# Which engine evicts the outputs: ScalarE in fixed stretches of the loop, VectorE elsewhere, and a branch hint on one more engine

## The chip, the core and the metric

The kernel runs on one core of a Trainium2 chip. Its engines are TensorE (PE; its weight loads are listed as PEld), VectorE (DVE), ScalarE (ACT), GpSimd (POOL) and SyncE (SP, which here issues nearly all transfers). The metric is the device time of one execution in microseconds. Three runs of the kernel before took 461.12, 462.41 and 466.04 us; their median is 462.41 us.

## The reference

Four batches of 12480 tokens with 128 features attend twice over 32 inducing points, and the result goes through a two-layer network with a squared ReLU. Cut to what is computed:

```python
def mab(q, kv):
    s = (q @ kv.transpose(0, 2, 1)) / sqrt(128)
    a = exp(s - s.max(-1, keepdims=True))
    a /= a.sum(-1, keepdims=True) + 1e-09
    return a @ kv
h = mab(I, x)                 # I: 32 inducing points, the same for all batches
y = mab(x, h)                 # so each row of y is a mixture of the 32 rows of h[b]
out = maximum(y @ w_in, 0) ** 2 @ w_out      # w_in 128x2048, w_out 2048x128
```

## The kernel before, in words

Since a row of y is a mixture of 32 rows, the kernel does not carry 2048 hidden columns per token. For each batch it turns the weights into a small quadratic form in the 32 attention weights: `prepare` (19 steps) computes `hw` (L466), the products `G` (L518), the sums `wq` on TensorE (L527), which `evac` writes to the batch's weights `w16` (L175 on ScalarE or L179 on VectorE), the linear part `lin` and `bias` (L591). These weights are "a batch's weights" below.

Four pieces of work run beside each other, batch by batch:

- `first(b)`: the first attention. Scores go to `sT` with their maximum (L298), the maxima are folded (`m` L305, a transposition `mt` on TensorE L307, `gm` L309, `gm` copied L311, a broadcast by TensorE `mb` L314, `nb` L316), `exp` on ScalarE (L323), a transposition `en` (L333), and `hacc` on TensorE (L345), which reads x once more from DRAM through five `xnb` buffers. `hq` (L351, L353) sums, and `hT` is done.
- `prepare(b)`, as above, needs `hT`.
- `second(b, G)`, seven groups per batch: scores, softmax on VectorE, GpSimd (L387, L394) and ScalarE (L388), then the 16-bit copy `a16` (L404 on ScalarE or L406 on VectorE) and its remainder (L407, VectorE), stored to DRAM.
- `squares(b, G)`: reads those back as `dT`, and adds squares `zz` (`sq` L442, `z` L448 on VectorE, L452 on GpSimd, stored into `dT` by L454).

The main loop goes over 104 chunks, 26 per batch, each of 480 columns. A chunk has four TensorE products into two double banks, `up` (L638, `hp`), two squarings on ScalarE of 128x960, `lift` (L647, `g`), and in the next round `down`: four products with `w16` and one with `lin` into one bank (`po`, L653 and L654, two buffers), the eviction of the bank with scale and bias to `o` (three buffers), and the store of `o` (L660). The eviction is L657 on ScalarE or L659 on VectorE. `g` has three buffers, so lifts can be at most three chunks ahead of `down`.

Which engine evicts is set by `to_act`: two running sums, `held["act"]` and `held["dve"]`, collect estimated nanoseconds of the work that was given to each engine, and a piece goes to ScalarE when its sum stays lower. The same test decides `a16` and the `w16` evictions. With it, ScalarE evicts 44 chunks and VectorE 60:

```
batch 0  chunks 0-25 ScalarE
batch 1  0-2 ScalarE, 3-7 VectorE, 8-19 ScalarE, 20-25 VectorE
batch 2  0-7 VectorE, 8-9 ScalarE, 10-14 VectorE, 15 ScalarE, 16-25 VectorE
batch 3  0-25 VectorE
```

The order of the background work is a plan: every step of the four pieces has a due time in chunks (`head` is the due time at which `prepare(b)` begins: -3.5, 13.9, 35 and 61), and `background` issues what is due after each lift. A scheduler (`schedule_with_timeline_sim`) then orders the instructions of each engine by its own estimate of durations. The engines run their lists in order.

At the end a flag is loaded on every engine (L933) and a branch (L934) skips a long other way of computing, "whole".

## Time and profile before

| what | value |
|---|---|
| runs, us | 461.12, 462.41, 466.04 |
| the profiled execution's own time | 464.73 us |
| its span, first to last instruction | 463.0 us |
| mean granted TensorE clock | 0.934 |
| VectorE busy | 325.7 us |
| ScalarE busy | 282.0 us |
| one output eviction, ScalarE / VectorE | 762 ns / 763 ns |
| the 60 evictions on VectorE | 45.4 us |
| the 44 evictions on ScalarE | 33.0 us |
| one lift of 128x960 | 974 ns |

The table's rows are totals over the span, and the limits differ along it. The text therefore reads stretches: for each batch the time from `hw` to the last `w16` (the "weights stage"), the stretch in which `first` streams x, and the last stretch, in which only chunks are left. In a chain of waits, "issue" is time in which nothing was waited for that the profile shows.

### The profile page before, as it was taken

Reading aid. Unit: us, or ns where it says so; the run is one execution under the profiler, and the core shown is the slowest. Engines: PE = TensorE matmul, PEld = TensorE weight load, DVE = VectorE, ACT = ScalarE, POOL = GpSimd, SP = SyncE. Lnnn points to the kernel's source line nnn. Section 1 sums busy time; section 2 is a strip of 40 time slices with the busy share of each in tenths; the row PEclk is TensorE's granted clock in tenths of the full one; section 3 lists DMA queues with packets and bytes.
Section 4 is the critical chain, followed back from the end, with each engine's and each line's share of the span. In section 5 each row is a group of like instructions: output and inputs, shape, how many; then the busy total and the mean of one; then the engine's idle time right before and its main releaser. Section 6 shows DMA issues by size and latency. Waiting matters only on the chain.

```text
span 463.0 us, 8566 instructions
## 1 busy us (share of the span) xinstructions
PE 366.8 (79%) x2979; PEld 163.2 (35%) x2979; DVE 325.7 (70%) x902; ACT 282.0 (61%) x397; POOL 85.9 (19%) x93
## 2 busy tenths in 40 slices
PE   0644744899979889878789888988879898788994
PEld 0003413543335333333244234433433344343441
DVE  8969378685643199497561899689626999996442
ACT  1004123479994497437567798566666878067993
POOL 1000011141210030232200132144100423340000
PEclk9999975699979799799599999999999999999998
DMA  7999980377759983667889958644794354337432
GB/s 296 421 248 392 372 295 24 97 240 249 207 173 337 335 277 101 197 188 187 266 276 293 344 195 244 195 138 145 240 290 154 102 167 165 101 128 231 151 136 105
DMA packets 64771, 100.71 MB, mean 218 GB/s; under 512 B 22992, under 2 KB 53968, under 8 KB 64720
## 3 DMA queue, kind: packets, MB, share of 16 engines
q1 hardware_dynamic: 64720, 100.09, 66.3%
q8 instruction: 25, 0.41, 0.4%
q14 instruction: 26, 0.21, 0.1%
HBM read 64.91 MB, written 31.95 MB: 209 GB/s over the span
## 4 chain that ended last, share of the span: by engine, by line
PE 30%; DVE 28%; DMA 26%; ACT 6%; issue 5%; SPq 2%; POOL 1%; ACTq 0%; DVEq 0%; POOLq 0%
DMA xnb<-xn_dram 8%; PE hp L638 8%; PE po L653 7%; ACT g L647 5%; DMA outT_dram<-o 5%; PE s L264 4%; PE hacc L345 4%; DMA xp_False<-xT_dram 4%; DMA dT<-zz 3%; DVE o L659 3%; DVE G L518 3%; DVE a L407 2%; PE wq L527 2%; DMA wo<-w_out_dram 2%; DMA dT<-ad 2%
## 5 line engine op out<-in xcount | busy, mean ns | idle before, releaser
L647 ACT ACTIVATE g<-hp 128x960 f16<-128x960 f32 x208 | 194.4, 974 | 60.7 <-PE hp L638 48.2
L638 PE MATMUL hp<-dT,pairs 96*128 96x480 f16 x416 | 121.4, 381 | 7.3 <-ACT g L647 4.9
L653 PE MATMUL po<-g,w 128*128 128x480 f16 x416 | 115.8, 377 | 7.6 <-ACT o L657 3.4
L387 POOL TENSOR_TENSOR e<-e,mx 128x480 f32<-128x480 f32 (+1 forms) x28 | 28.0, 999 | 232.2 <-DVE mx L383 76.3
L659 DVE TENSOR_SCALAR o<-po,osc,bias 128x480 f32<-128x480 f32 x60 | 45.4, 763 | 30.5 <-PE po L654 17.8
L653 PEld LDWEIGHTS <-w 128*128 128x128 f16 x416 | 40.6, 100 | 60.7 <-issue 19.3
L638 PEld LDWEIGHTS <-pairs 96*128 96x128 f16 x416 | 35.8, 101 | 66.6 <-issue 42.1
L345 PE MATMUL hacc<-xnb,en 128*32 128x128 f32 x784 | 38.3, 324 | 16.8 <-DMA xnb<-xn_dram 8.7
L264 PE MATMUL s<-xp_False,indT_sb 128*32 128x480 f32 (+1 forms) x224 | 32.9, 665 | 22.4 <-DMA xp_False<-xT_dram 12.1
L654 PE MATMUL po<-dT,lin 128*128 128x480 f16 x104 | 39.1, 379 | 7.7 <-DMA dT<-zz 7.5
L452 POOL TENSOR_TENSOR zz<-z 128x480 f16<-128x480 f32 (+1 forms) x28 | 30.2, 1078 | 66.3 <-DVE z L448 39.8
L323 ACT ACTIVATE sT<-sT,nb 128x480 f32<-128x480 f32 (+1 forms) x28 | 18.2, 658 | 33.5 <-DVE nb L316 33.5
L394 POOL TENSOR_TENSOR e<-e,z 128x480 f32<-128x480 f32 (+1 forms) x28 | 27.0, 967 | 56.1 <-DVE z L393 36.9
L345 PEld LDWEIGHTS hacc<-xnb,en 128*32 128x32 f32 x784 | 24.4, 126 | 33.6 <-DMA xnb<-xn_dram 9.7
L657 ACT ACTIVATE o<-po,bias,osc 128x480 f32<-128x480 f32 x44 | 33.0, 762 | 5.2 <-DMA outT_dram<-o 4.4
L353 DVE TENSOR_TENSOR hq<-hacc,hq 128x128 f32<-128x128 f32 x24 | 7.0, 291 | 37.6 <-PE hacc L345 37.6
L264 PE MATMUL s<-xp_False,hT 128*32 128x480 f32 (+1 forms) x224 | 27.7, 563 | 4.3 <-DVE k L195 1.4
L448 DVE TENSOR_SCALAR z<-sq,off,cut 128x480 f32<-128x480 f32 (+1 forms) x28 | 21.5, 767 | 9.3 <-PE sq L442 9.3
L518 DVE TENSOR_TENSOR G<-hwp,hw 128x512 f16<-128x512 f16 x64 | 24.9, 455 | 4.1 <-PE wq L527 4.1
L388 ACT ACTIVATE e<-e 128x480 f32<-128x480 f32 (+1 forms) x28 | 16.2, 578 | 17.0 <-POOL e L387 17.0
L404 ACT ACTIVATE a<-a,lessen 128x480 f16<-128x480 f32 (+1 forms) x20 | 13.6, 681 | 16.5 <-DVE a L397 16.3
L298 DVE TENSOR_SCALAR_CACHE_REDUCE sT<-s 128x480 f32<-128x480 f32 (+1 forms) x28 | 17.0, 608 | 9.1 <-PE s L264 9.1
(190 smaller groups left out, 419.2 us busy)
## 6 DMA issues: line engine op xcount, KB each, us to landing
outT_dram<-o SPq DMA_DIRECT2D x104, 240.0 KB, 2.8
xp_False<-xT_dram SPq DMA_DIRECT2D x24, 960.0 KB, 6.8
xnb<-xn_dram SPq DMA_DIRECT2D x28, 448.0 KB, 5.2
xnb<-xn_dram SPq DMA_DIRECT2D x24, 512.0 KB, 5.9
dT<-ad SPq DMA_DIRECT2D x72, 120.0 KB, 2.6
ad<-a SPq DMA_DIRECT2D x24, 240.0 KB, 2.5
dT<-zz SPq DMA_DIRECT2D x104, 30.0 KB, 2.3
wi<-w_in_dram SPq DMA_DIRECT2D x4, 512.0 KB, 5.6
```

What stands on the lines that cost most here:

```text
L264: nc.tensor.matmul(ps[32 * q:32 * q + 32, 0:w], lhsT, xp[:, w * q:w * q + w], start=True, stop=True,)
L345: st.last = nc.tensor.matmul(hacc[32 * q:32 * q + 32, 0:P], en[:, t], xg[:, t % 8], start=t < 4, stop=t + 4 >= nb32,)
L387: nc.gpsimd.tensor_tensor(e[:, 0:t], e[:, 0:t], mx[:, 0:t].unsqueeze(2).broadcast_to([P, t, MI]), op=ALU.subtract)
L394: nc.gpsimd.tensor_tensor(e[:, 0:t], e[:, 0:t], z[:, 0:t].unsqueeze(2).broadcast_to([P, t, MI]), op=ALU.mult)
L452: nc.gpsimd.tensor_tensor(g[rows], zv[rows], zv[rows], op=ALU.mult)
L518: tt(g[:, :, MI * j:MI * j + n], hwp[:, :, 0:n], hw16f[:, :, s0:s0 + n], op=ALU.mult)
L638: nc.tensor.matmul(hp[:, i, 0:CH].rearrange("p (q t) -> p q t", q=4), pairs[0:96, (2 * j + i) * P:(2 * j + i + 1) * P], self.dT[0:96], sta ...
L647: nc.scalar.activation(self.g[:, 2 * j:2 * j + 2], self.hp.pop(j)[:, 0:2, 0:CH], AF.Square)
L653: nc.tensor.matmul(po[:, 0:CH], st.w16[:, i], self.g[:, i], start=i == 0, stop=False)
L654: done = [nc.tensor.matmul(po[:, 0:CH].rearrange("p (q t) -> p q t", q=4), st.lin, self.dT, start=False, stop=True)]
L657: nc.scalar.activation(o, po[:, 0:CH], AF.Identity, bias=st.bias, scale=st.osc)
L659: done.append(nc.vector.tensor_scalar(o, po[:, 0:CH], st.osc, st.bias, op0=ALU.mult, op1=ALU.add))
```

## The change

`down` no longer asks `to_act`, it is told. A chunk is "heavy" if its number lies in one of the stretches of 18 chunks that begin at a batch's `head`, that is in -3.5 to 14.5, 13.9 to 31.9, 35 to 53 or 61 to 79; heavy chunks are evicted by ScalarE, all others by VectorE, and the very last by ScalarE. The evictions no longer enter the two sums, so the test for `a16` and `w16` comes out differently too: of the 28 `a16` copies 26 instead of 20 are on ScalarE, and all 16 `w16` evictions instead of 13. The list of instructions that get the branch hint now begins with the lift, so ScalarE gets one as well.

```diff
+HEAVY = 18
...
-            nc.scalar.activation(self.g[:, 2 * j:2 * j + 2], self.hp.pop(j)[:, 0:2, 0:CH], AF.Square)
+            return nc.scalar.activation(self.g[:, 2 * j:2 * j + 2], self.hp.pop(j)[:, 0:2, 0:CH], AF.Square)
...
-        def down(self):
+        def down(self, act):
...
-            if to_act(220 + 0.833 * CH, 110 + 1.042 * CH):
-                nc.scalar.activation(o, po[:, 0:CH], AF.Identity, bias=st.bias, scale=st.osc)
+            if act:
+                done.append(nc.scalar.activation(o, po[:, 0:CH], AF.Identity, bias=st.bias, scale=st.osc))
...
-    plan = []
+    plan, busy = [], []
+
+    def heavy(n):
+        return any(a <= n < z for a, z in busy)
...
+        busy.append((head, head + HEAVY))
...
-            chunk.lift(j)
+            done = [chunk.lift(j)]
...
-                done = chunks[n - 1].down()
+                done += chunks[n - 1].down(heavy(n - 1))
...
-    chunks[-1].down()
+    chunks[-1].down(True)
```

The engines' evictions after the change:

```
batch 0  chunks 0-25 ScalarE
batch 1  0-5 ScalarE, 6-8 VectorE, 9-25 ScalarE
batch 2  0 ScalarE, 1-8 VectorE, 9-25 ScalarE
batch 3  0 ScalarE, 1-24 VectorE, 25 ScalarE
```

ScalarE has 69 of them and VectorE 35. Up to chunk 2 of batch 1 nothing moves on any engine. Three places where the lists differ follow.

On VectorE, in batch 1 where `first` of batch 2 folds its maxima (`o_3` and `o_4` are the outputs of chunks 3 and 4, `gm` the folded maxima, `mx`, `z` and `e` belong to the last groups of `second`). Before:

```order
L391 TENSOR_REDUCE z_1_5_2243<-e_1_5_2202 128x15
L659 TENSOR_SCALAR o_3_2517<-po_3_2511,osc_157,bias_158 128x480
L381 STREAM_TRANSPOSE e_1_6_2285<-s_1_6_2279 128x256
L309 TENSOR_REDUCE gm_2293<-mt_2291 1x32
L392 TENSOR_SCALAR z_1_5_2243<-z_1_5_2243 128x15
L383 TENSOR_REDUCE mx_1_6_2287<-e_1_6_2285 128x8
L311 COPY gm_2_2295<-gm_2293 1x128
L393 RECIPROCAL z_1_5_2243<-z_1_5_2243 128x15
L659 TENSOR_SCALAR o_4_2567<-po_4_2561,osc_157,bias_158 128x480
L448 TENSOR_SCALAR z_2_2407<-sq_2_2402,off_153,cut 128x480
L316 TENSOR_SCALAR nb<-mb_2301 128x1
```

and after:

```order
L392 TENSOR_REDUCE z_1_5_2243<-e_1_5_2202 128x15
L382 STREAM_TRANSPOSE e_1_6_2285<-s_1_6_2279 128x256
L310 TENSOR_REDUCE gm_2293<-mt_2291 1x32
L393 TENSOR_SCALAR z_1_5_2243<-z_1_5_2243 128x15
L384 TENSOR_REDUCE mx_1_6_2287<-e_1_6_2285 128x8
L312 COPY gm_2_2295<-gm_2293 1x128
L394 RECIPROCAL z_1_5_2243<-z_1_5_2243 128x15
L449 TENSOR_SCALAR z_2_2407<-sq_2_2402,off_153,cut 128x480
L317 TENSOR_SCALAR nb<-mb_2301 128x1
```

The two evictions ahead of and behind `gm` are gone from this list. On TensorE, `mb` also moves: it stood behind the products `hp_6_0` and the first two of `po_5`, and now stands ahead of them.

On ScalarE at the same place, up to the exponentials `sT` of `first` of batch 2. Before:

```order
L647 ACTIVATE g_4_2506<-hp_4_1_2483 128x960
L657 ACTIVATE o_2_2456<-po_2_2450,bias_158,osc_157 128x480
L647 ACTIVATE g_5_2556<-hp_5_0_2508 128x960
L647 ACTIVATE g_5_2556<-hp_5_1_2540 128x960
L647 ACTIVATE g_6_2583<-hp_6_0_2558 128x960
L388 ACTIVATE e_1_6_2285<-e_1_6_2285 128x256
L647 ACTIVATE g_6_2583<-hp_6_1_2580 128x960
L323 ACTIVATE sT_1809,zs_2321<-sT_1809,nb 128x480 x6
```

and after:

```order
L648 ACTIVATE g_4_2506<-hp_4_1_2483 128x960
L658 ACTIVATE o_2_2456<-po_2_2450,bias_158,osc_157 128x480
L658 ACTIVATE o_3_2517<-po_3_2511,bias_158,osc_157 128x480
L648 ACTIVATE g_5_2556<-hp_5_0_2508 128x960
L648 ACTIVATE g_5_2556<-hp_5_1_2540 128x960
L658 ACTIVATE o_4_2567<-po_4_2561,bias_158,osc_157 128x480
L389 ACTIVATE e_1_6_2285<-e_1_6_2285 128x256
L648 ACTIVATE g_6_2583<-hp_6_0_2558 128x960
L324 ACTIVATE sT_1809,zs_2321<-sT_1809,nb 128x480 x6
```

Two evictions come in ahead of the exponentials, and one lift, `g_6` of `hp_6_1`, moves behind them.

On ScalarE at the end of the weights stage of batch 3 (`w_1<-wq_0` to `wq_3` are the four `w16` evictions; the `g` numbers are chunks, first of batch 2, then of batch 3). Before:

```order
L647 ACTIVATE g_25_4647<-hp_25_1_4632 128x960
L388 ACTIVATE e_3_3_4445<-e_3_3_4445 128x480
L647 ACTIVATE g_0_4677<-hp_0_0_4649 128x960
L647 ACTIVATE g_0_4677<-hp_0_1_4667 128x960
L647 ACTIVATE g_1_4695<-hp_1_0_4679 128x960
L647 ACTIVATE g_1_4695<-hp_1_1_4692 128x960
L647 ACTIVATE g_2_4725<-hp_2_0_4697 128x960
L647 ACTIVATE g_2_4725<-hp_2_1_4720 128x960
L175 ACTIVATE w_1_151<-wq_0_4168,tsg 128x128
L388 ACTIVATE e_3_4_4543<-e_3_4_4543 128x480
L388 ACTIVATE e_3_5_4627<-e_3_5_4627 128x480
L647 ACTIVATE g_3_4772<-hp_3_0_4727 128x960
```

and after:

```order
L648 ACTIVATE g_25_4647<-hp_25_1_4632 128x960
L658 ACTIVATE o_24_4658<-po_24_4652,bias_147,osc_146 128x480
L648 ACTIVATE g_0_4677<-hp_0_0_4649 128x960
L176 ACTIVATE w_1_151<-wq_2_4279,tsg 128x128
L389 ACTIVATE e_3_5_4627<-e_3_5_4627 128x480
L648 ACTIVATE g_0_4677<-hp_0_1_4667 128x960
L658 ACTIVATE o_25_4688<-po_25_4682,bias_147,osc_146 128x480
L405 ACTIVATE a_3_4_4578<-a_3_4_4576,lessen 128x480
L648 ACTIVATE g_1_4695<-hp_1_0_4679 128x960
L176 ACTIVATE w_1_151<-wq_3_4322,tsg 128x128
L648 ACTIVATE g_1_4695<-hp_1_1_4692 128x960
```

Before, three chunks of batch 3 were lifted ahead of the first of the four evictions. After, the last of them stands behind the first lift of chunk 1: three lifts fewer lie ahead of the finished weights.

## The prediction, made before the changed kernel was run

> **What bounds the kernel now.** I read the page's busy times first, then its slices, then the busy times by stretch, then the chain that ended last.
>
> ```profile
> PE 366.8 (79%) x2979; PEld 163.2 (35%) x2979; DVE 325.7 (70%) x902; ACT 282.0 (61%) x397; POOL 85.9 (19%) x93
> DVE  8969378685643199497561899689626999996442
> ACT  1004123479994497437567798566666878067993
> ```
>
> No engine is the limit throughout. From the 32nd to the 36th of the 40 slices (11.6 us each) VectorE is full, and in the 35th ScalarE falls to 0. The stretches (start and end, length, busy time by engine) say where each limit lies:
>
> ```profile
> 161.00:211.00 50.00, 42.55 (x355) 18.32 (x348) 42.97 (x125) 31.37 (x46) 12.73 (x12) 0.93 0.61 191
> 255.00:305.00 50.00, 44.75 (x380) 19.75 (x372) 42.48 (x121) 38.94 (x56) 12.00 (x12) 1.00 0.75 240
> 305.00:327.00 22.00, 17.94 (x142) 7.04 (x138) 20.46 (x55) 15.28 (x28) 9.99 (x9) 1.00 0.41 126
> 327.00:352.00 25.00, 21.80 (x245) 10.46 (x241) 9.52 (x24) 15.13 (x18) 0.99 (x1) 1.00 0.88 277
> 353.00:408.00 55.00, 47.05 (x365) 21.99 (x363) 53.85 (x143) 34.02 (x44) 16.66 (x16) 0.97 0.39 123
> ```
>
> The columns after the length are PE, PEld, DVE, ACT, POOL, then the granted clock, the DMA share and GB/s. The first, second and fifth are the weights stages of batches 1, 2 and 3. In the first two no engine is full (DVE 42.97 and PE 44.75 of 50 are the busiest). In the third VectorE works 53.85 of 55 us and ScalarE 34.02: this stage is VectorE's, with 21 us of ScalarE free. The fourth streams x and is the transfers' (DMA share 0.88). The chain shows the ends of the third stage and of the kernel:
>
> ```profile
> 353.79 0.63 DVE hw L466
> 391.88 0.23 DVE bias L591
> 407.32 0.26 DVE w L179
> 440.79 13.78 ACT g L647 x15
> 456.29 0.78 DVE o L659
> ```
>
> From the last `w16` at 407.3 us on ScalarE's lifts set the pace, 13.78 us for 15, so 0.92 us each, until the last output.
>
> **Prices.** Moving an eviction costs ScalarE what it frees on VectorE:
>
> ```profile
> L657 ACT ACTIVATE o<-po,bias,osc 128x480 f32<-128x480 f32 x44 | 33.0, 762 | 5.2 <-DMA outT_dram<-o 4.4
> L659 DVE TENSOR_SCALAR o<-po,osc,bias 128x480 f32<-128x480 f32 x60 | 45.4, 763 | 30.5 <-PE po L654 17.8
> L404 ACT ACTIVATE a<-a,lessen 128x480 f16<-128x480 f32 (+1 forms) x20 | 13.6, 681 | 16.5 <-DVE a L397 16.3
> L175 ACT ACTIVATE w<-wq,tsg x13: 350/368/388, 85.7 to 394.1; 128x128 f16<-128x128 f32 x13
> ```
>
> So 25 evictions more on ScalarE are 19.1 us there, six `a16` 4.1 us, three `w16` 1.1 us: 24.3 us in all, and about as much less on VectorE. Three places decide what that is worth.
>
> The Trainium skill speaks against the move: its page "ScalarE: Activation LUTs", section "Rules for kernel authors", tells to use VectorE for additions and products, up to about 3 times faster there in bf16. By that the 13 evictions of term C would free VectorE some 3 us, an estimate, instead of the measured sum below. The trace disagrees here: 762 and 763 ns for the same shape from PSUM in fp32.
>
> **Term A, batch 1 before x is streamed: -3.5 us.** Rows of the timeline (start, length, in brackets the wait before it):
>
> ```profile
> 217.78 1.87 ACT L647 ACTIVATE g<-hp 128x960 f16<-128x960 f32 x2
> 221.53 0.78 DVE L659 TENSOR_SCALAR o<-po,osc,bias 128x480 f32<-128x480 f32 x1 [3.95 <-DMA dT<-zz]
> 222.58 0.24 DVE L309 TENSOR_REDUCE gm<-mt 1x32 f32<-1x128 f32 x1
> 223.25 0.98 PE L638 MATMUL hp<-dT,pairs 96*128 96x480 f16 x2
> 224.96 0.58 PE L314 MATMUL mb<-every,gm 1*128 1x1 f32 x2
> 227.36 0.69 ACT L323 ACTIVATE sT<-sT,nb 128x480 f32<-128x480 f32 x1
> 231.75 1.07 PE L345 MATMUL hacc<-xnb,en 128*32 128x128 f32 x30
> ```
>
> VectorE stood 3.95 us in front of the eviction of chunk 3, and `gm` stood behind it. With the eviction gone from its list `gm` can be done before 219 us, and `mb`, now ahead of `hp_6_0` at 223.25, at about 223.3 instead of 224.96; the exponentials' input `nb` is ready at about 224.0. ScalarE takes the wait over. Eviction 3 ends at about 222.3, the two lifts that ran at 217.78 now follow until 224.1, then eviction 4 (0.76), one exponential of 0.41 and one lift, and the exponentials start at about 226.2, 1.2 us earlier than 227.36. On VectorE the eviction of chunk 5 goes as well, and `sq_3`, which `z_3` waits for, stands earlier on TensorE; so `en` follows the first exponential directly, and `hacc` starts at about 228, not 231.75. That is 3.5 us or a little more, and streaming follows it, since `hacc` frees the buffers that are loaded next. Lower bound of the time: the whole wait, `gm` 5.0 us earlier. Upper: if the exponentials, queued behind two more evictions, gain nothing from `nb`, two evictions late, +1.5 us. I take -3.5, the step that I could follow row by row.
>
> The Trainium skill, page "PSUM — Partial Sum Buffer", section "Engine vs sequencer instructions", calls ScalarE's and VectorE's queues strict FIFO; the trace agrees (`gm` 222.58 behind the wait that ended at 221.53). By that rule each wait for one of the three `o` buffers now holds lifts instead of softmax, which is the slow rival's mechanism.
>
> **Term B, weights stage of batch 2 and what follows (255 to 327): 0 us.** Seven evictions (batch 1 chunks 20 to 25, batch 2 chunk 0) go to ScalarE. The chain holds three of them:
>
> ```profile
> 309.39 0.51 DVE o L659
> 311.14 0.69 DVE o L659
> 318.14 0.57 DVE o L659
> ```
>
> 1.8 us at most, 2.3 with whole durations: the lower end. In 255 to 305 TensorE is the busiest and stays so. In 305 to 327 ScalarE has 15.28 of 22 us, gets three evictions (2.3) and about one chunk that the new order leaves behind the weights (1.9): 19.5, just below VectorE, which falls from 20.46 to 18.2. Unhidden, the seven cost 5.3 us: the upper end. I take 0, since the gain on VectorE and the lag on ScalarE are of one size.
>
> **Term C, weights stage of batch 3: -2 us.** What leaves VectorE in this stage:
>
> ```profile
> L659 DVE TENSOR_SCALAR o<-po,osc,bias 128x480 f32<-128x480 f32 x13 | 9.8, 754 | 2.2 <-DMA outT_dram<-o 2.2
> L406 DVE TENSOR_SCALAR a<-a,lessen 128x480 f16<-128x480 f32 x5 | 2.3, 461 | 0.0
> L179 DVE TENSOR_SCALAR w<-wq,tsg 128x128 f16<-128x128 f32 x3 | 1.0, 339 | 0.0
> ```
>
> 13.1 us, so 53.85 becomes 40.75. ScalarE gets 13 x 0.762 + 5 x 0.681 + 3 x 0.368 = 14.4 us and loses the three lifts that now come after the weights (2.9): 34.02 becomes 45.5. TensorE keeps about 45. If VectorE still ended the stage with the 7.0 us of idle time that it had in batch 1, it would last 47.75 us, 7.2 less. If ScalarE, now the busiest, has the 5.3 to 7.0 us idle that the busiest engines of the other two stages had, it lasts 50.8 to 52.5, so 4.2 to 2.5 less. I take 5, between, nearer to ScalarE. Against it stand the three lifts (3 x 0.92 = 2.8) and one eviction (0.76) that now lie in the last stretch: +3.5. Some of the lifts' idle time there should go, as VectorE enters it with less undone:
>
> ```profile
> L647 ACT ACTIVATE g<-hp 128x960 f16<-128x960 f32 x46 | 42.4, 968 | 6.4 <-PE hp L638 4.3 <-PE po L653 1.7
> ```
>
> I count 0.5 of these 6.4 us. Sum -5 + 3.5 - 0.5 = -2. Lower end -7.2, if the late lifts cost nothing; upper +1, 2.5 gained and 3.5 paid back. What hides the evictions on ScalarE is its free 21 us; without that cover they cost 9.9.
>
> **The tail: 0 us.** After the output come the branch and the end:
>
> ```profile
> L934 ACTq COMPARE_BRANCH  x1: 50/50/50, 455.0 to 455.0; - x1
> L934 ACTq EVENT_SEMAPHORE  x1: 17/17/17, 457.5 to 457.5; - x1
> L934 SPq COMPARE_BRANCH  x1: 70/70/70, 458.1 to 458.1; - x1
> L934 SPq EVENT_SEMAPHORE  x8: 17/17/17, 461.0 to 461.6; - x8
> L966 SPq BRANCH_PREFETCH_HINT  x1: 46/46/46, 450.7 to 450.7; - x1
> ```
>
> ScalarE without a hint needs 2.5 us from branch to next instruction, SP with one 2.8. ScalarE branches at about 457.2 now, behind the last eviction, and would go on at 459.7 even without a hint, before SP's 461.0. The last eviction costs the same on either engine. Bounds: 0 to -2.8, if the hints of the other engines sped SP up; nothing shows that.
>
> **Sum.** -3.5 + 0 - 2 + 0 = -5.5 us. Against its own time the profiled execution goes from 464.73 (span 463.0 and 1.7 around it) to 459.2; it stands 2.3 above the median of the runs, to which I apply the same difference: 462.4 - 5.5 = 456.9 us.
>
> **Rivals.**
>
> *ScalarE becomes the bound* (slower). Place: the two stages of B and C, where a chunk on ScalarE grows from two lifts (1.94) to 2.70 us plus exponentials. For it: 45.5 us of work against 40.75 on VectorE in C, and in-order queues, which turn each late bank into a late lift. Against it: in 255 to 305 ScalarE evicted eight chunks already and had 11 us free. Price: A nothing, B +5.3, C +1: 468.7 us. It decides once ScalarE's busy share passes about 95% in either stage.
>
> *The gain is taken back* (within 1%). A's head start ends in a stretch that the transfers pace (DMA 0.88 in the like stretch of batch 2), and C's 5 us are paid back by the lifts. Price: about -1, 461.4 us.
>
> *VectorE's whole relief comes through* (much faster). C -7.2, B -2.3, A -5.0: 447.9 us. For it: VectorE ended most of the chain in 353 to 408. Against it: PE at 47.05 of 55 there.
>
> *The hint does nothing.* It changes no number above, since ScalarE's end is covered by SP's.
>
> **How the numbers follow.** About 1% (4.6 us) is what a measurement of this kernel can tell from no change. Forecast 0.45, with 0.38 beyond 1% and 0.07 within, for its 5.5 us are only just over the bound; ScalarE the bound 0.18, slower; taken back 0.23, within; full relief 0.14, faster. Faster 0.52, within 0.30, slower 0.18. The forecast's own range is 452 to 460. With the rivals at 447.9 and 468.7, and no more than 2 in 10 left out, I give 449.5 to 466.0.
>
> **What would show it.** Right: `hacc` of batch 2 about 3.5 us earlier; from `hw` to the last `w16` of batch 3 about 49 us instead of 53.8, VectorE at 41 and ScalarE at 45 us of it; the last `w16`, now on ScalarE, followed by 49 lifts instead of 46. Wrong: a stage of 53 us or more with ScalarE full (slow rival); `hacc` no earlier (A fails at ScalarE's wait); ScalarE's branch gap still 2.5 us (hint).

## The result, and the profile after it

The changed kernel took 448.58 us (median of 4 runs, 443.4 to 452.13) beside 461.76 us for the kernel before (4 runs, 461.07 to 466.04). The ratio is 0.9658, with a 95% interval of 0.9548 to 0.9769: 3.4% faster, where 456.9 us was forecast. A second series of six runs gave 0.9761 (0.9724 to 0.9799), 11.1 us less (9.3 to 12.8). So the gain is 11 to 16 us, two to three times the 5.5 that were forecast. Executions over 1.5% above the fastest of their kernel count as disturbed and are left out of the ratios, so that a ratio need not be that of the medians beside it, and some rest on few executions: two of six for C alone, the hint alone and the smaller dose on ScalarE, three of twelve for B and C, three of six for 14 chunks, 22 chunks and less on ScalarE.

The page after, busy times and two of the slice rows:

```profile
PE 356.2 (80%) x2979; PEld 159.2 (36%) x2979; DVE 313.7 (70%) x868; ACT 301.9 (67%) x431; POOL 85.7 (19%) x93
DVE  8959459777563189589563899879534999894441
ACT  1004104269997698555777798799759998997894
```

VectorE and ScalarE now stand at nearly the same total. The 0 that ScalarE had in the 35th slice is gone.

The two profiled executions differ more than the medians: spans of 463.0 and 447.4 us. Of these 15.6 us, 3.4 lie ahead of `hw` of batch 1 (161.2 against 157.8 us), where the change had moved nothing yet. From one execution to the next that point lay anywhere from 156 to 165 us in the kernels below. So stages are compared by their lengths, not by their dates. Before, by events: `hw` to the last `w16` of batch 2, from there to `hacc` of batch 3, from there to `hw`, from there to the last `w16`, from there to the last output (columns as in the prediction):

```profile
255.13:304.52 49.39, 44.14 (x369) 19.58 (x361) 42.00 (x121) 38.33 (x54) 11.58 (x11) 1.00 0.76 242
304.50:325.30 20.80, 17.20 (x109) 6.22 (x108) 19.26 (x52) 14.08 (x26) 10.06 (x9) 1.00 0.39 120
325.30:353.70 28.40, 24.74 (x285) 11.95 (x285) 11.90 (x29) 16.83 (x22) 1.34 (x2) 1.00 0.84 267
353.71:407.24 53.53, 45.98 (x359) 21.48 (x357) 52.40 (x140) 34.02 (x44) 16.66 (x16) 0.97 0.39 122
407.24:456.30 49.06, 45.95 (x230) 21.05 (x230) 30.05 (x62) 42.63 (x47) 7.12 (x8) 1.00 0.50 164
```

The same five after:

```profile
248.65:295.96 47.31, 43.39 (x369) 19.26 (x362) 43.94 (x123) 39.27 (x57) 14.17 (x13) 1.00 0.80 264
296.00:314.20 18.20, 17.05 (x105) 6.45 (x103) 15.82 (x41) 17.59 (x30) 5.82 (x8) 1.00 0.43 135
314.20:342.50 28.30, 25.23 (x281) 12.37 (x284) 10.58 (x26) 19.56 (x26) 1.60 (x2) 0.94 0.82 252
342.51:389.63 47.12, 42.47 (x360) 20.11 (x352) 45.16 (x123) 42.32 (x62) 17.39 (x17) 1.00 0.44 139
389.63:441.00 51.37, 48.52 (x246) 22.11 (x245) 29.48 (x56) 46.28 (x54) 7.48 (x8) 1.00 0.49 162
```

The reader should see four things. The weights stage of batch 2 lost 2.1 us and the stretch to `hacc` 2.6; in that stretch the fullest engine changed from VectorE (19.26 of 20.8) to ScalarE (17.59 of 18.2). The stretch that streams x kept its length. The weights stage of batch 3 lost 6.4 us, with VectorE at 45.16 and ScalarE at 42.32. The last stretch grew by 2.3. So B's region gave 4.7 us and C's 4.1 net, by these two profiles; that a region got shorter does not yet say that its part did it, and the kernels without one part come to that.

A's place, in the timeline after:

```profile
214.38 0.23 DVE L310 TENSOR_REDUCE gm<-mt 1x32 f32<-1x128 f32 x1
217.69 0.75 ACT L658 ACTIVATE o<-po,bias,osc 128x480 f32<-128x480 f32 x1 [3.24 <-DMA outT_dram<-o]
219.26 0.58 PE L315 MATMUL mb<-every,gm 1*128 1x1 f32 x2
221.84 0.72 ACT L324 ACTIVATE sT<-sT,nb 128x480 f32<-128x480 f32 x1
225.64 1.07 PE L346 MATMUL hacc<-xnb,en 128*32 128x128 f32 x30
```

`gm` no longer stands behind an eviction. The wait for an `o` buffer has gone to ScalarE (3.24 us), as forecast. From the last `w16` of batch 1 to `hacc` of batch 2 it takes 19.05 us instead of 21.69.

The branch at the end, after:

```profile
L939 ACTq COMPARE_BRANCH  x1: 68/68/68, 441.8 to 441.8; - x1
L939 ACTq EVENT_SEMAPHORE  x1: 17/17/17, 445.0 to 445.0; - x1
L939 SPq COMPARE_BRANCH  x1: 70/70/70, 442.8 to 442.8; - x1
L939 SPq EVENT_SEMAPHORE  x8: 17/17/17, 445.5 to 446.0; - x8
```

ScalarE, now with a hint, needs 3.2 us across the branch, where it needed 2.5 without one. SP needs 2.7, about as before (2.9).

### The profile page after: what moved, and what is told of

It reads as the page before. It is cut to its first block, busy times and chain, and to the rows that moved or that the text cites. A ratio compares the mean times of both kernels' runs of the same rounds, so it can differ in the third digit from the quotient of the medians.

```text
span 447.4 us, 8577 instructions
## 1 busy us (share of the span) xinstructions
PE 356.2 (80%) x2979; PEld 159.2 (36%) x2979; DVE 313.7 (70%) x868; ACT 301.9 (67%) x431; POOL 85.7 (19%) x93
## 4 chain that ended last, share of the span: by engine, by line
PE 31%; DMA 27%; DVE 27%; ACT 7%; issue 4%; SPq 2%; POOL 1%; DVEq 0%; ACTq 0%; POOLq 0%
DMA xnb<-xn_dram 9%; PE hp L639 9%; PE po L654 7%; ACT g L648 6%; DMA wo<-w_out_dram 6%; DVE G L519 4%; DMA dT<-zz 4%; DMA outT_dram<-o 4%; PE s L265 4%; PE hacc L346 4%; DVE a L408 2%; PE po L655 2%; DMA dT<-ad 2%; PE wq L528 2%; DVE e L382 2%
## 5 line engine op out<-in xcount | busy, mean ns | idle before, releaser
L658 ACT ACTIVATE o<-po,bias,osc 128x480 f32<-128x480 f32 x69 | 51.8, 760 | 7.3 <-DMA outT_dram<-o 5.8
L346 PE MATMUL hacc<-xnb,en 128*32 128x128 f32 x784 | 35.6, 305 | 19.5 <-DMA xnb<-xn_dram 11.9
L265 PE MATMUL s<-xp_False,indT_sb 128*32 128x480 f32 (+1 forms) x224 | 32.8, 664 | 21.7 <-DMA xp_False<-xT_dram 12.0
L660 DVE TENSOR_SCALAR o<-po,osc,bias 128x480 f32<-128x480 f32 x35 | 26.9, 773 | 24.7 <-PE po L655 18.2
L324 ACT ACTIVATE sT<-sT,nb 128x480 f32<-128x480 f32 (+1 forms) x28 | 18.3, 661 | 34.1 <-DVE nb L317 34.1
L453 POOL TENSOR_TENSOR zz<-z 128x480 f16<-128x480 f32 (+1 forms) x28 | 29.0, 1034 | 63.6 <-DVE z L449 43.1
L346 PEld LDWEIGHTS hacc<-xnb,en 128*32 128x32 f32 x784 | 22.4, 118 | 36.3 <-DMA xnb<-xn_dram 12.3
L519 DVE TENSOR_TENSOR G<-hwp,hw 128x512 f16<-128x512 f16 x64 | 26.7, 479 | 5.4 <-PE wq L528 5.4
L405 ACT ACTIVATE a<-a,lessen 128x480 f16<-128x480 f32 (+1 forms) x26 | 17.6, 679 | 14.6 <-DVE a L398 13.0
L408 DVE SCALAR_TENSOR_TENSOR a<-a,lessen,a 128x480 f16<-128x480 f32 (+1 forms) x28 | 21.5, 767 | 1.8 <-ACT a L405 1.8
```

The lines of the kernel that those rows point to most:

```text
L265: nc.tensor.matmul(ps[32 * q:32 * q + 32, 0:w], lhsT, xp[:, w * q:w * q + w], start=True, stop=True,)
L346: st.last = nc.tensor.matmul(hacc[32 * q:32 * q + 32, 0:P], en[:, t], xg[:, t % 8], start=t < 4, stop=t + 4 >= nb32,)
L408: nc.vector.scalar_tensor_tensor(a16[:, 1, 0:w], a[:, 0:w], lessen, a16[:, 0, 0:w], op0=ALU.add, op1=ALU.subtract)
L453: nc.gpsimd.tensor_tensor(g[rows], zv[rows], zv[rows], op=ALU.mult)
L519: tt(g[:, :, MI * j:MI * j + n], hwp[:, :, 0:n], hw16f[:, :, s0:s0 + n], op=ALU.mult)
L658: done.append(nc.scalar.activation(o, po[:, 0:CH], AF.Identity, bias=st.bias, scale=st.osc))
```

## The experiments

The theory was that each of the three places gives its own share, because evictions leave the engine that ends the stage there. The first rival was that only batch 3 matters, where VectorE was full; another, that the hint or the order of the work does it.

For the parts, three tables take the place of the tests: the chunks that ScalarE evicts (numbered 0 to 103), and the `a16` and `w16` that VectorE makes. The three parts alone and A with B have no hint on ScalarE and the last eviction on VectorE, as before; the change without one part has both, as the change. With all evictions on ScalarE, the hint that stands behind an eviction goes to ScalarE and VectorE has none:

```diff
+ON_ACT = [...]        # before: (0, 29), (34, 46), (60, 62), (67, 68); change: (0, 32), (35, 53), (61, 79), (103, 104)
+A16_DVE = [...]       # before: (2, 6), (3, 0) to (3, 6); change: (3, 5), (3, 6)
+W16_DVE = [...]       # before: (3, 1), (3, 2), (3, 3); change: none
-        return any(a <= n < z for a, z in busy)
+        return any(a <= n < z for a, z in ON_ACT)
-            if to_act(120 + 0.833 * w, 110 + 1.042 * w):
+            if (b, G) not in A16_DVE:
```

Every microsecond of gain below is one minus the ratio times the median of before in the same series (460.44, 463.29, 463.75 and 460.82 us in the four series), with the interval in brackets. In these series the change itself ran only in the second, where it gained 11.1 us. So what is said of a kernel of the third or fourth series against the change is the difference of two such gains.

### The parts alone

**A alone.** Chunks 29 to 31 added to ScalarE's table of before, 34 taken out:

```diff
-ON_ACT = [(0, 29), (34, 46), (60, 62), (67, 68)]
+ON_ACT = [(0, 32), (35, 46), (60, 62), (67, 68)]
```

> Only the evictions of batch 1 around the fold of batch 2's maxima are changed: chunks 3 to 5 go to ScalarE and chunk 8 to VectorE; all other evictions, a16 and w16 stay on the engine they had, and the hint stays as it was. Theory (each place gives its own share): hacc of batch 2 starts about 3 us earlier than before, counted from the end of the weights of batch 1, and the time falls by 2 to 4 us. Rival (only the full VectorE of batch 3 matters): hacc may come earlier, but the time is within 1 us of before, because the stretch that streams x absorbs it.

Measured: 458.01 us, ratio 0.9918 (0.9858 to 0.9978), 3.8 us less (1.0 to 6.5). From the last `w16` of batch 1 to `hacc` 18.8 us instead of 21.7. The theory's size; the rival that only batch 3 counts falls here, though only just, as the interval begins at 1.0. How the stretch passes its 2.9 us on is not shown: from the last `w16` of batch 1 to `hw` of batch 2, behind the stream of x, it takes 43.9 us instead of 45.1, so 1.2 less. One thing was not foreseen: the stretch between the last `w16` of batch 2 and `hacc` of batch 3, where no eviction was moved, is shorter too:

```profile
296.80:314.50 17.70, 15.53 (x97) 6.17 (x96) 15.67 (x43) 14.42 (x25) 7.63 (x7) 1.00 0.37 109
```

17.7 us, as short as with B. Two lifts fewer lie ahead of the last `w16` there (105 instead of 107), and VectorE had less of its other work left (15.67 us instead of 19.26). So the length of that stretch alone doesn't show what B does.

**B alone.**

```diff
-ON_ACT = [(0, 29), (34, 46), (60, 62), (67, 68)]
+ON_ACT = [(0, 29), (34, 53), (61, 62), (67, 68)]
```

> Only the evictions of chunks 20 to 25 of batch 1 and 0 of batch 2 go to ScalarE and chunk 8 of batch 2 to VectorE, all else as before. Theory: from hw of batch 2 to hacc of batch 3 it takes 65 to 67 us instead of 70.2, and the time falls by 3 to 5 us. Rival (only the full VectorE of batch 3 matters): under 1 us. The prediction's own term was 0, with -2.3 and +5.3 as bounds.

Measured: 460.2 us, ratio 0.9984 (0.9929 to 1.0039), 0.7 us less (-1.8 to 3.3). The stretch became as short as expected (65.7 us from `hw` to `hacc`), but the time did not follow: alone, B is worth nothing that could be measured.

**C alone.**

```diff
-ON_ACT = [(0, 29), (34, 46), (60, 62), (67, 68)]
+ON_ACT = [(0, 29), (34, 46), (60, 79)]
-A16_DVE = [(2, 6), (3, 0), (3, 1), (3, 2), (3, 3), (3, 4), (3, 5), (3, 6)]
-W16_DVE = [(3, 1), (3, 2), (3, 3)]
+A16_DVE = [(3, 5), (3, 6)]
+W16_DVE = []
```

> Only what lies in the weights stage of batch 3 is changed: chunks 9 to 25 of batch 2 and chunk 0 of batch 3 on ScalarE, a16 and w16 as in the change. Theory: hw to the last w16 of batch 3 47 to 49 us instead of 53.5, the stretch after it about 2 us longer, and the time falls by 3 to 5 us. Rival (only the full VectorE of batch 3 matters): this part alone gives nearly the whole gain, 10 us or more. The prediction's term was -2.

Measured: 460.78 us, ratio 0.9902 (0.9821 to 0.9983), 4.5 us less (0.8 to 8.2). The size of the theory, and not the whole gain. The stage took 51.3 us, longer than expected.

**The hint alone.**

```diff
-            chunk.lift(j)
+            done = [chunk.lift(j)]
```

> Only the branch hint on ScalarE is added; every engine's other instructions stand in the order they had. Prediction: 0, since ScalarE goes on before SyncE does in any case; in the profile ScalarE's gap from branch to next instruction stays at 2.5 to 3.2 us. Rival: a hint on every engine lets all of them go on earlier, SyncE too, and the time falls by 1 to 2.8 us.

Measured: 465.31 us, ratio 0.9984 (0.9905 to 1.0063): no gain that could be measured. The interval, from 2.9 us more to 4.4 less, does not exclude the rival's 1 to 2.8 by itself; the rows speak against it. ScalarE's in this kernel:

```profile
L940 ACTq COMPARE_BRANCH  x1: 68/68/68, 457.4 to 457.4; - x1
L940 ACTq EVENT_SEMAPHORE  x1: 17/17/17, 459.9 to 459.9; - x1
```

2.5 us, as without the hint. SP's gap stays at 2.9.

### The parts together, and the change without one part

**The change once more.** No edit.

> The changed kernel once more, unedited, for a narrower interval and as the partner of the three kernels beside it. Expected: 10 to 16 us under the kernel before. In its profile the time up to hw of batch 1, where nothing has moved yet, again differs by up to 3 us from one execution to the next, while the lengths of the stages behind it repeat within 1.5 us.

Measured: 451.33 us, ratio 0.9761 (0.9724 to 0.9799), 11.1 us less. The stages of batch 3 repeat within 0.1 us (28.6 and 18.5 us), but that of batch 1 did not: 45.5 us here and 48.8 in the first profile. The last section comes back to that.

**A and B, without C.**

```diff
-ON_ACT = [(0, 29), (34, 46), (60, 62), (67, 68)]
+ON_ACT = [(0, 32), (35, 53), (61, 62), (67, 68)]
```

> Both earlier parts together (evictions of chunks 3 to 5 and 20 to 25 of batch 1 and 0 of batch 2 on ScalarE, chunk 8 of batches 1 and 2 on VectorE), the weights stage of batch 3 and the copies as before. Each alone gave -3.8 us (-6.5 to -1.0) and -0.7 us (-3.3 to +1.8). Theory that the places simply add: 3 to 6 us faster than before. Rival, that the parts only pay together because what one saves ahead of the weights is given back in the chunks behind them as long as batch 3 keeps VectorE full: 0 to 3 us faster.

Measured: 456.17 us, ratio 0.9829 (0.9782 to 0.9876), 7.9 us less (5.7 to 10.1). More than either expected.

**A and C, without B.**

```diff
-ON_ACT = [(0, 32), (35, 53), (61, 79), (103, 104)]
+ON_ACT = [(0, 32), (35, 46), (60, 79), (103, 104)]
```

> The change without its part B: chunks 20 to 25 of batch 1 and 0 of batch 2 on VectorE and chunk 8 of batch 2 on ScalarE as before, all else as in the change. If the parts add as they measured alone (A -3.8, C -4.5, B -0.7): 8 to 12 us faster than before, about as fast as the changed kernel. If B was the mis-sized term (0 counted, 4 us worth): only 5 to 9 us faster than before, and from hw of batch 2 to hacc of batch 3 it takes 68 us or more instead of 65.5.

Measured: 454.38 us, ratio 0.9877 (0.9831 to 0.9924), 5.7 us less (3.5 to 7.8). B was the mis-sized term by the time. Its second sign failed: `hw` of batch 2 to `hacc` of batch 3 took 66.4 us, not 68, where the change takes 65.6 and 65.4; without B that region is nearly as short. By the profile what is missing lies in batch 3, where from `hw` to the last output it takes 101.6 us instead of 98.5 and 98.0, with the weights stage 2.9 us longer. But the granted clock was 0.93 in that stage here and 1.00 in both profiles of the change, with as many instructions on VectorE (123) and the same work (45.64 us and 45.16), while TensorE was busy for 45.55 us instead of 42.47. A clock of 0.93 lengthened a stage of like size by 3 us in kernels that do the same work in it (last section). So this profile does not show where B's gain lies.

**B and C, without A.**

```diff
-ON_ACT = [(0, 32), (35, 53), (61, 79), (103, 104)]
+ON_ACT = [(0, 29), (34, 53), (61, 79), (103, 104)]
```

> The change without its part A: chunks 3 to 5 of batch 1 on VectorE and chunk 8 on ScalarE as before, all else as in the change. If the parts add, A being worth 3 to 4 us: 8 to 10 us faster than before, with the stretch from the last w16 of batch 1 to hacc of batch 2 back at 21 to 22 us instead of 18.6 to 19. If the transfers of the next stretch swallow A's head start (the prediction's rival that the gain is taken back): within 1.5 us of the changed kernel.

Measured: 460.51 us, ratio 0.984 (0.9783 to 0.9897), 7.4 us less (4.7 to 10.0). By that A is worth 3.7 us in its place too, as the theory had it. The sign in the profile failed: from the last `w16` of batch 1 to `hacc` of batch 2 it took 19.8 us, not 21 to 22, beside 19.1 and 18.6 in the change. To `hw` of batch 2 it is 43.5 us without A, and 42.1 and 43.5 with it. So that the transfers leave A its head start is likely by the times, and not shown by the profiles.

Alone the parts sum to 3.8 + 0.7 + 4.5 = 9.0 us. Each as the difference between the change (11.1) and the change without it: A 11.1 - 7.4 = 3.7 (+-3.2), B 11.1 - 5.7 = 5.4 (+-2.8), C 11.1 - 7.9 = 3.2 (+-2.8). B is the one part for which the two answers lie apart, 0.7 and 5.4 with intervals that barely overlap. That B pays only beside another part is likely, not shown.

### Is it the evictions or the copies, and how far can it go?

**The evictions without the copies.** The change's chunks, with `a16` and `w16` as before:

```diff
-A16_DVE = [(3, 5), (3, 6)]
-W16_DVE = []
+A16_DVE = [(2, 6), (3, 0), (3, 1), (3, 2), (3, 3), (3, 4), (3, 5), (3, 6)]
+W16_DVE = [(3, 1), (3, 2), (3, 3)]
```

> The change's evictions and its hint, but a16 and w16 on the engines that they had before: eight a16 and three w16 of the last groups on VectorE, instead of two a16. Theory (VectorE's load in the weights stage of batch 3 decides): about 3.3 us of work come back to VectorE, which is 96% busy there, so the stage from hw to the last w16 of batch 3 lasts 48.5 to 50.5 us instead of 47.1, and the gain over before shrinks by 1 to 3 us. Rival (the evictions alone carry the gain): no difference from the changed kernel beyond 1 us.

Measured: 449.3 us, ratio 0.9703 (0.9671 to 0.9734), 13.8 us less, so 2.7 us (+-2.3) better than the change in the same series and as good as the change in its first. The theory had it 1 to 3 us worse, the rival within 1 us. The copies do not carry the gain; the evictions do.

**All evictions on ScalarE.**

```diff
-ON_ACT = [(0, 32), (35, 53), (61, 79), (103, 104)]
+ON_ACT = [(0, 104)]
```

> All 104 evictions on ScalarE, a16 and w16 as in the change. This moves 35 more evictions, 26.9 us, from VectorE to ScalarE. ScalarE would then work 328 us and VectorE 287. Theory that ScalarE is the limit wherever chunks are all that is left: the last stretch of the kernel, where ScalarE is busy 46.3 of 51.4 us with 24 evictions on VectorE, gets 18 us more and grows by 13 us or more; in all the kernel is 10 to 20 us slower than the changed one, about as slow as before or slower. Rival (ScalarE still has room everywhere): within 3 us of the changed kernel.

Measured: 469.61 us, ratio 1.0069 (1.0026 to 1.0113), 3.2 us slower than before and 14.3 slower than the change. As the theory said: ScalarE does become the bound if it is given more. In the profile it was busy for 66.7 of the 70.9 us of the last stretch.

**Fewer and more chunks per stretch.**

```diff
-HEAVY = 18
+HEAVY = 14
```

> The changed kernel with 14 chunks instead of 18 per stretch: 16 more evictions stay on VectorE (chunks 2 to 5 of batch 1, four around the end of the weights stages of batches 0 and 2, and chunks 75 to 78 in that of batch 3). Theory (VectorE's load ahead of the fold and in the weights stages costs): the part of batch 1 is undone (3 us) and about 3 us of evictions come back into the stage of batch 3, so 4 to 8 us slower than the changed kernel. Rival (ScalarE is already the tighter engine and the change moved too much): faster than the changed kernel by 1 to 4 us.

Measured: 458.86 us, ratio 0.9855 (0.9779 to 0.9932), 6.7 us less than before, so 4.4 (+-4.0) worse than the change.

```diff
-HEAVY = 18
+HEAVY = 22
```

> The changed kernel with 22 chunks instead of 18 per stretch: eleven more evictions (8.4 us) on ScalarE, of chunks 6 to 8 of batch 1, 1 to 4 of batch 2 and 1 to 4 of batch 3. Theory (ScalarE is at its limit between the last w16 of batch 2 and hacc of batch 3, 17.6 of 18.2 us, and near it in the last stretch, 46.3 of 51.4): that stretch grows by 2 to 3 us, the last one by 0 to 2, in all 1 to 5 us slower than the changed kernel. Rival (more relief of VectorE goes on paying): 1 to 4 us faster.

Measured: 462.25 us, ratio 0.9897 (0.9815 to 0.9979), 4.8 us less than before, 6.3 (+-4.2) worse than the change, a little past the expectation. In the profile the stretch to `hacc` grew by 4.8 us and the last one by 11.4, with six lifts more left for it, where 2 to 3 and 0 to 2 were expected; the weights stage of batch 2 (44.7 us) and the stream of x (23.4) got shorter. With 14, 18 and 22 chunks the gains are 6.7, 11.1 and 4.8: the change's number is better than 14 and 22 on either side.

### Which engine sets the weights stage of batch 3

The stretch from `hw` to `bias` in three profiles: before, with A and B but not C, and after:

```profile
353.70:391.90 38.20, 33.96 (x237) 14.61 (x236) 38.01 (x104) 31.79 (x41) 11.21 (x11) 1.00 0.39 129
```
```profile
341.30:378.20 36.90, 34.62 (x247) 14.89 (x240) 36.68 (x101) 31.34 (x40) 10.61 (x11) 1.00 0.39 128
```
```profile
342.50:371.10 28.60, 25.11 (x204) 10.99 (x197) 28.34 (x81) 26.37 (x39) 11.04 (x10) 1.00 0.36 118
```

VectorE is 99% busy in each, and the length follows its work: 38.01, 36.68, 28.34 us. It looks as if VectorE alone sets this stretch, and as if its load were the price. Two doses test that.

**7.7 us more on VectorE.** Sixteen products `G` of batch 3 are written twice more with the same values:

```diff
-                tt(g[:, :, MI * j:MI * j + n], hwp[:, :, 0:n], hw16f[:, :, s0:s0 + n], op=ALU.mult)
+                for _ in range(3 if b == 3 and c < 2 else 1):
+                    tt(g[:, :, MI * j:MI * j + n], hwp[:, :, 0:n], hw16f[:, :, s0:s0 + n], op=ALU.mult)
```

> The changed kernel with 16 products G of batch 3 done three times over instead of once (the eight of the first two groups, written again with the same values): 16 x 0.479 = 7.7 us more on VectorE ahead of bias of batch 3, nothing more on ScalarE. Theory (VectorE alone sets the time from hw to bias, since it was 99% busy there in every profile so far): hw to bias grows from 28.6 to 35.5 to 37 us. Lifts run on meanwhile until they are six into batch 3 (162 of 208) and then stand, as they stood before the change from bias to the last w16; so of the 7.7 us about 3 come back as lifts done ahead of the weights and the kernel is 3 to 6 us slower than the changed one. Rival (TensorE or ScalarE set that stage as well, and VectorE's load counts only in part): hw to bias grows by less than 4 us.

Measured: 450.72 us, ratio 0.9737 (0.9685 to 0.9789): 1.1 us less than the change (+-3.0), not 3 to 6 more. The stretch:

```profile
340.80:373.90 33.10, 29.76 (x227) 13.05 (x220) 32.42 (x98) 31.00 (x45) 11.13 (x10) 1.00 0.36 120
```

VectorE is full again, and the stretch grew by 4.4 us, between the theory's bounds and the rival's: its work there rose by 4.1 us, so some 3.6 us of other work went behind `bias`. And the weights' delay was paid for in lifts. The count of ScalarE's lifts from the last `w16` to the last output (the busy time and the number are those of lifts alone), after and with the dose:

```profile
389.63:441.00 51.37, 45.47 (x50) 1.00 0.49 162
```
```profile
390.50:443.20 52.70, 42.56 (x46) 0.97 0.48 158
```

Of the 50, one began ahead of the window, so 49 and 46 are left. The last `w16` came 2.6 us later, counted from `hw` (49.7 against 47.1), with three lifts fewer to do. In this one profile the last stretch was slow (52.7 us for 46 lifts, at a clock of 0.97), which the timed runs don't show as a loss. **The theory in its strict form falls** by the second series: VectorE sets when the weights are done, but a later date seems to be nearly repaid as long as ScalarE and TensorE go on with chunks meanwhile. Against the change's 15.8 us in its first series the dose would have cost 3.6 us (+-5.6), which decides nothing.

**7.6 us more on ScalarE.** Ten evictions are done twice:

```diff
-                done.append(nc.scalar.activation(o, po[:, 0:CH], AF.Identity, bias=st.bias, scale=st.osc))
+                for _ in range(2 if self.b == 2 and 13 <= self.c < 23 else 1):
+                    done.append(nc.scalar.activation(o, po[:, 0:CH], AF.Identity, bias=st.bias, scale=st.osc))
```

> The changed kernel with ten evictions of batch 2 (chunks 13 to 22) done twice on ScalarE: 10 x 0.760 = 7.6 us more on ScalarE in the weights stage of batch 3, nothing more on VectorE. Theory (VectorE alone sets the time from hw to bias; ScalarE, 26.3 of 28.6 us busy there, has about 2 us free): hw to bias stays within 1.5 us of 28.6, but fewer lifts are done by the last w16 (153 to 156 instead of 159), and these come back in the last stretch at about 1.05 us each: 2 to 6 us slower than the changed kernel. Rival (ScalarE hides evictions there at no cost, as the term C of the prediction had it): within 1 us of the changed kernel.

Measured: 462.79 us, ratio 1.0048 (0.9994 to 1.0102), 13.3 us (+-3.1) slower than the change, about as slow as before. `hw` to `bias` stayed at 28.9 us and 155 lifts were done by the last `w16`, both as the theory had it. The price is over twice what it gave; four lifts more in the last stretch, at 1.05 us each, are 4.2 us of it. The dose is not of ScalarE's time alone: an eviction done twice also holds its `po` bank, of which there are two, 0.76 us longer, and no run separates the two.

**3.8 us more on ScalarE.** As above with `13 <= self.c < 18`.

> The changed kernel with five evictions of batch 2 (chunks 13 to 17) done twice on ScalarE, 3.8 us more there, half of the earlier dose of 7.6 that cost some 10 to 13 us. If ScalarE's cost is in proportion (1.3 to 1.7 us for each us added): 5 to 7 us slower than the changed kernel. If ScalarE still had 2 to 3 us free and the cost begins past them: 0 to 3 us slower.

Measured: 458.78 us, ratio 0.9837 (0.9775 to 0.9899), 3.6 us (+-3.4) slower than the change. Here too 155 lifts were done by the last `w16`. Between the two expectations: about 1 us for each added one, within an interval from nearly 0 to 2, and more than that past it.

**Less on ScalarE.**

```diff
-ON_ACT = [(0, 32), (35, 53), (61, 79), (103, 104)]
+ON_ACT = [(0, 32), (35, 53), (61, 64), (65, 68), (69, 72), (73, 76), (77, 79), (103, 104)]
```

with the copies as before.

> The change with less on ScalarE in the weights stage of batch 3: chunks 12, 16, 20 and 24 of batch 2 evicted by VectorE, and a16 and w16 on the engines that they had before the change: 3.0 + 5.2 = 8.2 us back to VectorE. If ScalarE is the tighter engine there and the change went past the best point: 1 to 4 us faster than the changed kernel, so 13 to 17 us faster than before. If VectorE's load sets the stage after all: 3 to 6 us slower than the changed kernel.

Measured: 454.46 us, ratio 0.9793 (0.9736 to 0.985), 9.5 us less than before; 1.5 us (+-3.2) slower than the change. Neither can be seen: taking 8.2 us from ScalarE, about 7 at VectorE's prices, brought nothing, and a cost of up to 4.7 us is not excluded.

So on the side of VectorE the optimum is flat for 7 to 8 us, as far as these intervals tell, and on ScalarE's side it is steep. No version here beats the change by more than the two series of the change lie apart.

## Why the prediction was wrong

The direction was right. The time was just below the range, and the gain two to three times the forecast. By its steps:

- **What bounds the kernel.** Right: no engine throughout, VectorE in the weights stage of batch 3. The prices held too (760 and 773 ns for an eviction after the change). They are for fp32 from PSUM and say nothing against a factor for bf16, which no run here has.
- **A, -3.5 us.** Right by the times: 3.8 alone and 3.7 (+-3.2) in its place. `mb` stood where it was put (219.26, ahead of `hp_6_0`), ScalarE took the wait over. Counted from the last `w16` of batch 1, `hacc` came 2.6 us earlier, and 3.1 in the second profile, a little less than 3.5; that the stream of x passes this on is not shown.
- **B, 0 us. This is the step that failed**, at "I take 0, since the gain on VectorE and the lag on ScalarE are of one size". In the change B is worth 5.4 us (+-2.8), beyond the lower end of -2.3 that the chain gave; no other term was measured outside its own bounds. ScalarE's part was foreseen: three evictions and two lifts more between the last `w16` and `hacc`. What they were set against was wrong twice. The sum's 19.5 is below VectorE's 20.46 of before, but above the 18.2 to which VectorE falls, so by its own numbers the stretch should have become about 1 us shorter. And the window of 22 us ran 1.7 us past `hacc`; counted to `hacc`, ScalarE had 14.08 us, and 14.08 + 2.3 + 1.9 is 18.3, where VectorE's 19.26 in 20.8 had set the length. ScalarE at 17.59 of 18.2 then gave a stretch 2.6 us shorter, though it was as full as the slow rival asked for. For 255 to 305 it said that TensorE stays the busiest. It did not quite: VectorE has 43.94 us after and TensorE 43.39, and the stage lost 2.1 us, with 25 lifts done in it instead of 27. A busiest engine at 89% was no bound here. Yet this working explains only why 0 was too little for the place, and not the 5.4 us: alone B is worth 0.7 us, and without it the two stretches of its place take 66.4 us together instead of the change's 65.6 and 65.4. So the sum failed in counting B as a term of its own, apart from A and C. How B pays beside them stays open.
- **C, -2 us.** Right in sign, too small in size, though its intervals hold the 2: 4.5 alone, 3.2 in its place, 4.1 in the profile. The stage gave 6.4 instead of 5, and the late lifts cost 2.3 where +3.5 - 0.5 was counted. VectorE did not fall to 40.75 but to 45.16: it took up other work of the stage in the freed time, and the 16 products `G` took 8.5 us instead of 7.3. ScalarE rose to 42.3 instead of 45.5. The sentence on ScalarE's free 21 us as cover was right, and the doses show its edge: past the change there is hardly any left.
- **The tail and the hint, 0.** Right: nothing that could be measured alone, and no shorter gap on ScalarE (2.5 us alone, 3.2 in the change).
- **The rivals.** "VectorE's whole relief", 447.9 us, came nearest, at a chance of 0.14. Its time was right by luck: it counted 7.2 us for C and 2.3 for B, where 3.2 to 4.5 and 5.4 were measured, and with 7.7 us put back on VectorE the gain stayed. "ScalarE becomes the bound" was the right mechanism at the wrong amount. It is what happens with more evictions (22 chunks, all, the doses). "The gain is taken back" is out as a whole; of A's head start it may hold in part. "The hint does nothing" was right.

What replaces the strict theory is the balance between the date of the last `w16` and the lifts then left. For batch 3, from `hw`, by the profiles (lifts counted by their starts; the granted clock up to the last `w16` and behind it):

| kernel | `hw` to last `w16`, us | lifts left | `hw` to last output, us | clock |
|---|---|---|---|---|
| before | 53.5 | 46 | 102.6 | 0.97, 1.00 |
| A alone | 55.4 | 46 | 104.5 | 1.00, 1.00 |
| B alone | 54.1 | 46 | 103.3 | 0.94, 1.00 |
| A and B | 54.4 | 46 | 107.0 | 0.94, 0.94 |
| C alone | 51.3 | 49 | 104.5 | 0.97, 0.97 |
| A and C | 50.0 | 50 | 101.6 | 0.93, 1.00 |
| B and C | 51.5 | 50 | 103.5 | 0.90, 1.00 |
| the change | 47.1 | 49 | 98.5 | 1.00, 1.00 |
| the change again | 47.1 | 49 | 98.0 | 1.00, 1.00 |
| evictions without copies | 47.9 | 46 | 97.5 | 1.00, 1.00 |
| 7.7 us more on VectorE | 49.7 | 46 | 102.4 | 1.00, 0.97 |
| less on ScalarE | 46.4 | 46 | 95.9 | 1.00, 1.00 |
| 3.8 us more on ScalarE | 46.8 | 53 | 106.0 | 0.96, 0.97 |
| 7.6 us more on ScalarE | 49.4 | 53 | 111.1 | 0.93, 0.94 |
| 22 chunks | 47.1 | 55 | 109.9 | 1.00, 0.97 |

These are single profiles, and rows of unlike clocks cannot be told apart by a few microseconds. Nor does batch 3 decide alone: with less on ScalarE it was shortest, and the kernel was no faster than the change.

Before, ScalarE was six lifts into batch 3 and then started none from `bias` to the last `w16`, for 15.3 us. VectorE had put evictions ahead of the weights that those lifts then waited for. The row for lifts in that stretch (the one counted began ahead of it):

```profile
391.90:407.20 15.30, 0.65 (x1) 0.89 0.38 107
```

After, nine lifts run in the 18.5 us from `bias` to the last `w16`. That stall is what C's gain seems to be made of; no run takes it away by itself. Three things stay open. Why B pays beside the other parts and not alone: its own place is hardly longer without it, and the one profile that has batch 3 longer has a lower clock there. The scheduler reorders the whole rest of the program with each table, so the experiments tell what each table is worth, with its order, and not an eviction with the order held. And why the second 3.8 us on ScalarE cost more than the first.

## What to carry to other kernels

When work moves from a full engine to another, set the receiver's new sum against the length of the stretch, cut at the event that ends it, and not at a round number behind it. That a stretch got shorter is not yet the moved work's doing: here one did so in a kernel in which none of its own work had moved. A delay of what the pipeline waits for seems to count only as far as the pipeline runs dry; count the units left at that moment as well as its date. After a move, test both sides with a dose: here 7.7 us on the relieved engine cost nothing that could be measured and 7.6 us on the receiver cost 13. And read the granted clock of a stretch before its length.

## What the runs showed of the hardware

**The clock falls in some executions and not in others.** The weights stage of batch 1 took 48.8 us in one profile of the changed kernel and 45.5 in the other. Three rows of 3 us from each, first the slower, at the place where they part:

```profile
183.00:186.00 3.00, 2.71 (x11) 1.33 (x12) 1.39 (x2) 2.08 (x3) 0.95 (x1) 0.76 1.06 286
186.00:189.00 3.00, 3.00 (x15) 0.95 (x13) 1.84 (x10) 1.32 (x2) 0.92 (x2) 0.50 1.01 349
189.00:192.00 3.00, 3.00 (x24) 1.71 (x20) 1.38 (x5) 1.68 (x2) 0.10 (x1) 0.60 0.18 30
```
```profile
183.00:186.00 3.00, 2.59 (x16) 1.48 (x16) 1.26 (x2) 1.99 (x3) 0.89 (x2) 1.00 1.04 281
186.00:189.00 3.00, 3.00 (x30) 1.44 (x28) 2.86 (x15) 2.51 (x4) 1.15 (x2) 1.00 1.01 364
189.00:192.00 3.00, 2.52 (x21) 1.02 (x19) 3.00 (x8) 2.48 (x5) 0.00 (x0) 1.00 0.53 100
```

The granted clock drops to half for some 6.8 us of these nine, and the stage is 3.3 us longer. It is not the change: in all 18 profiles this stage has nearly the same work (346 to 349 TensorE products, 120 or 121 instructions on VectorE), and it took 45.5 to 46.0 us in the ten with a granted clock of 1.00 there, 48.5 to 48.9 in the five with 0.93, the kernel before among them, and 51.4 to 51.9 in the three with 0.87. The Trainium skill, page "TensorE: Matmul & The Clock Gate", section "Part 1: The HAM clock gate (the "warmup" mystery)", describes this: half clock after an idle window of about 3.4 us, and a window that runs free of the kernel, so that the outcome varies from run to run. The rows agree in the 0.50; a whole idle window they do not show, for in the 3.4 us ahead of the drop TensorE was busy for 1.4 us and its longest pause was 2.0 (1.8 in the profile without the drop). One such dip is worth a fifth to a third of what the change brought, so two profiles alone cannot settle a few microseconds.

**One kind of VectorE instruction takes three times as long beside GpSimd.** `least_d` takes a minimum of two tiles in SBUF; its row after (shortest, median, longest in ns):

```profile
L411 DVE TENSOR_TENSOR least_d<-least_d,a x28: 265/401/1200, 80.1 to 399.2; 128x480 f16<-128x480 f16 x24, 128x240 f16<-128x240 f16 x4
```

The four of 1180 to 1200 ns, and one of 820, each began while GpSimd was in one of its products of 128x480 (`e` or `zz`); those of 400 ns had none beside them. The Trainium skill's page "SBUF — State Buffer", section "Who interferes with whom", says that a VectorE instruction with two inputs in SBUF contends with a GpSimd instruction that reads SBUF. The trace agrees, at 0.8 us a time. In the profile before, three minima beside a `zz` took 390 ns, and there the `zz` took 1.7 to 1.8 us instead of its median of 1.0: which of the two is longer differs from case to case.
